# A gated feed-forward behind linear attention on one core: a first strip of 576 tokens, batch 1 by token, and later loads moved by a strip

## The chip, the cores and the metric

The kernel runs on one core of a Trainium2 chip. A core has TensorE (PE in the profile; PEld is its weight load), VectorE (DVE), ScalarE (ACT), GpSimd (POOL) and SyncE (SP), which run side by side and each take their instructions in order. The metric is the device time of one execution in microseconds, as the median of several runs. The profile is of one execution, with times from the start of its span.

## The reference

For each of 8 batches and 8 heads, with 576 tokens of 64 numbers, `kv` sums over the tokens, `q` is multiplied by it, each token's 64 results are divided by their root mean square and scaled by `g_norm`. The eight heads of a token side by side are a row of `x` (4608 x 512). Then comes a gated feed-forward of width 1536.

```python
kv = np.einsum('bhsd,bhse->bhde', k, v)
out = np.einsum('bhsd,bhde->bhse', q, kv)
rms = np.sqrt(np.mean(out * out, axis=-1, keepdims=True) + 1e-06)
attn = out / rms * g_norm
x = attn.transpose(0, 2, 1, 3).reshape(B * S, H * D)
y = ((x @ w_a) * (x @ w_b)) @ w_out
```

## The kernel before, in words

**Feed-forward.** The 4608 tokens are cut into 9 strips of 512. `xt` holds x transposed (channels in the partitions, 4 blocks of 128 channels). In a strip, a unit (class `Unit`, `ffn_ab`) makes 128 of the 1536 columns: 4 products with `wa_t` into one PSUM bank, copied by ACT to `a_sb` (L373), then 4 products with `wb_t` into another bank, which DVE multiplies with the copy into `abt` (L377). Twelve units, n = 0 to 11, are followed by four output groups of 128 tokens, n = 12 to 15 (`ffn_o`): 12 products with `wo_t` each, a copy by DVE or ACT in turn (L431, L429), and stores issued by SP (L409). All products go through `product` (L161), which cuts each into two with 64 columns of weights where `halves` is set.

**Attention.** The 576 tokens of a batch are not aligned with the strips: batch b begins at token 576 b, strip s at 512 s. Batches 0 and 1 (`EARLY`) are loaded by POOL per pair of heads (`load_heads`, L119), with q transposed by PE (`qtr`) and kv made by PE (`kv1`). Their x is made per pair with channels in the partitions: product with q (`px`, or `x` with the block-diagonal `kvb`), square on ACT (`psq`), sum over channels by a product with `ones` and reciprocal root on ACT (`pss`, L233), scaling on DVE into `xt` (`pst`, L243). Batch 0 does this at the head, batch 1 between the half groups of strip 0's output.

**Batches 2 to 7, by token.** `load_late` (L137 to L150) issues six DMAs on POOL: q, in two, to a DRAM tile `qs` in bf16, k and v, each with its last 64 tokens apart. A small copy to `gate` makes POOL wait for the last but one batch's q transpose first. `transpose_q` (L154) is a transposing DMA issued by SP from `qs` to `qT`. PE then makes kv into bank 7 (`kv`, L178, 40 products), a copy gives `kvs` (L618), and `tx` (L293, 40 products) makes x with tokens in the partitions: four chunks of 128 tokens in banks 4 to 7, a last chunk (`LC`) of 64 in two other banks, copied off by ACT (L304). Each chunk then takes `tsq` (square, ACT L310), `tss` (sum over 64, DVE L314), `trs` (reciprocal root on ACT L323, then its product with `g_all` on POOL L330) and `txt` (product, DVE L339, and a transposing DMA on SP into `xt`, L343).

**What sets the order.** The program is written out by hand, and each engine takes its part of it in order. In strip s, `slot(A, s, n)` places the steps of batch s + 1 after unit or group n, and in the middle of it for halves: with k0 = 5, 1, 4, 0, 4, 0 in strips 1 to 6 for kv (in strips 3 and 5 for two batches at once) and x0 = 6.5, 2.5, 5.5, 0.5, 5.5, 0.5 for tx. Loads of a batch are issued two batches ahead at n = 14, 10, 14, 8 of strips 1 to 4; those of batch 2 follow batch 1's at the head, those of batch 3 come at n = 3 of strip 1.

**Loads at the head.** POOL issues batch 0's later pairs, then the weights `wa_t` and `wb_t` in blocks of 256 columns (L477, L130, L131), `wo_t` in 12 pieces (L134), then batch 1's pairs and batch 2. Eight such DMAs are in flight at once; a ninth waits for the first (rows such as "POOL wo_t L134 <- DMA wb_t" in the view of the waits).

## Time and profile before

| what | us |
|---|---|
| median of 3 runs (312.43 to 312.77) | 312.49 |
| profiled execution | 312.61 |
| its span | 310.8 |
| PE busy, first product of the feed-forward to last product | 14.1 to 307.6 |
| strip 0, units | 14.10 to 35.15 |
| strip 0, output groups with batch 1 between | 35.15 to 49.96 |
| strip 1 | 49.96 to 82.75 |
| granted TensorE clock, as a share of full speed | 1.0 |

A line of a timeline gives the start and the duration in us, the engine, the line of the kernel and the operation with what it writes and reads; "x12" is the number of instructions that it merges. Products overlap, so a group's end is some 0.17 us behind the start of the next. In the view of the DMA issues the last number is the time from issue to landing in us. The clock was granted in full in every stretch, so durations may be carried from one stage to another.

### The profile page before, as it was taken

How to read it: one execution, taken by the hardware profiler on the slowest of the kernel's cores; microseconds unless marked ns; L12 is line 12 of the kernel's file. 1: busy time of each engine (PE TensorE's matmuls, PEld its weight loads, DVE VectorE, ACT ScalarE, POOL GpSimd, SP SyncE). 2: the span in 40 equal slices, each digit the busy share in tenths (PEclk: the TensorE clock that was granted, in tenths of full speed). 3: DMA queues.
4: the chain of work that ended last, by engine and by line, in shares of the span. 5: the costliest groups of instructions: out<-in, count | busy, mean ns of one | idle time of the engine just before them, and what ended most of it. 6: DMA issues, size and time to landing. Idle time of an engine off the chain costs nothing.

```text
span 310.8 us, 6542 instructions
## 1 busy us (share of the span) xinstructions
PE 304.3 (98%) x2684; PEld 157.6 (51%) x2701; DVE 140.6 (45%) x235; ACT 117.0 (38%) x231; POOL 101.3 (33%) x123
## 2 busy tenths in 40 slices
PE   7899999999999999999999999999999999999996
PEld 3444476655555555555555555444444444444444
DVE  4544335458248603484386123752782143214321
ACT  3743255354255313551564034632651233123310
POOL 8954991093274630043646300221240000000000
PEclk9999999999999999999999999999999999999999
DMA  8999999999899999047998990073021200030002
GB/s 180 197 196 199 201 188 168 161 169 184 174 137 185 139 174 193 2 84 134 178 177 118 162 188 2 19 160 110 20 51 42 103 1 0 34 103 0 0 36 101
DMA packets 94403, 36.29 MB, mean 117 GB/s; under 512 B 64934, under 2 KB 89894, under 8 KB 94374
## 3 DMA queue, kind: packets, MB, share of 16 engines
q0 software_dynamic: 59120, 18.44, 56.6%
q1 hardware_dynamic: 34786, 16.93, 25.0%
q10 hardware_dynamic: 468, 0.51, 0.6%
q8 instruction: 21, 0.34, 0.5%
q14 instruction: 8, 0.07, 0.1%
HBM read 37.78 MB, written 12.98 MB: 163 GB/s over the span
## 4 chain that ended last, share of the span: by engine, by line
PE 79%; DMA 12%; POOL 7%; issue 1%; ACT 0%; POOLq 0%
PE P L161 77%; DMA wb_t<-in_moe_w_b_dram 6%; DMA vtl<-in_v_dram 4%; DMA wo_t<-in_moe_w_out_dram 2%; PE P L293 1%; PE P L178 1%; POOL vt L119 1%; POOL qt L119 1%; POOL qs L142 1%; POOL kt L119 1%; POOL wa_t L477 0%; POOL wb_t L477 0%; POOL wo_t L134 0%; POOL ktl L145 0%; POOL vtl L145 0%
## 5 line engine op out<-in xcount | busy, mean ns | idle before, releaser
L377 DVE TENSOR_TENSOR ab<-P,asb 128x512 bf16<-128x512 f32 x108 | 74.4, 691 | 103.2 <-PE P L161 99.9
L161 PE MATMUL P<-xt,wb_t 128*64 128x512 bf16 (+1 forms) x641 | 111.4, 379 | 0.2
L161 PE MATMUL P<-xt,wa_t 128*64 128x512 bf16 (+1 forms) x636 | 111.0, 379 | 0.6 <-issue 0.2
L373 ACT CAST asb<-P 128x512 bf16<-128x512 f32 x108 | 63.1, 586 | 89.6 <-PE P L161 89.5
L161 PE MATMUL P<-wo_t,ab 128*64 128x512 bf16 (+3 forms) x673 | 95.5, 371 | 0.3
L161 PEld LDWEIGHTS <-ab 128*64 128x64 bf16 (+1 forms) x678 | 47.5, 106 | 45.0
L161 PEld LDWEIGHTS <-wa_t 128*64 128x64 bf16 (+1 forms) x644 | 46.0, 106 | 46.2 <-issue 0.6
L161 PEld LDWEIGHTS <-wb_t 128*64 128x64 bf16 (+1 forms) x644 | 45.8, 106 | 45.8
L330 POOL TENSOR_TENSOR sqt<-rst,g_all 128x512 f32<-128x512 f32 (+1 forms) x24 | 25.0, 1046 | 83.0 <-ACT rst L323 83.0
L429 ACT COPY osb<-P 128x512 f32<-128x512 f32 x17 | 10.0, 586 | 70.2 <-PE P L161 60.2
L431 DVE COPY osb<-P 128x512 f32<-128x512 f32 x18 | 12.4, 691 | 44.9 <-PE P L161 40.4
L142 POOL DMA_DIRECT2D qs<-in_q_dram x12 | 19.8, 1654 | 0.7 <-issue 0.3
L314 DVE TENSOR_REDUCE sst<-sqt 128x8 f32<-128x512 f32 (+1 forms) x24 | 16.3, 680 | 1.7 <-ACT sqt L310 1.5
L339 DVE TENSOR_TENSOR qv<-P,sqt 128x512 bf16<-128x512 f32 x18 | 12.3, 681 | 0.0
L330 POOL TENSOR_TENSOR k_x<-rst,g_all 128x512 f32<-128x512 f32 x6 | 6.3, 1044 | 17.4 <-ACT rst L323 17.4
L323 ACT ACTIVATE rst<-sst,eps_t 128x8 f32<-128x8 f32 (+1 forms) x30 | 9.0, 300 | 7.2 <-DVE sst L314 7.0
L310 ACT ACTIVATE sqt<-P 128x512 f32<-128x512 f32 x18 | 10.5, 585 | 0.1
L243 DVE SCALAR_TENSOR_TENSOR xt<-P,g_col,rs 128x288 bf16<-128x288 f32 x16 | 7.5, 511 | 5.1 <-ACT rs L233 5.1
L134 POOL DMA_DIRECT2D wo_t<-in_moe_w_out_dram x12 | 6.4, 530 | 6.7 <-DMA wb_t<-in_moe_w_b_dram 3.2
L233 ACT ACTIVATE rs<-P,eps_t 128x576 f32<-128x576 f32 (+1 forms) x9 | 6.1, 689 | 3.7 <-PE P L161 3.4
L139 POOL COPY gate<-qT 1x1 bf16<-1x1 bf16 x5 | 0.9, 177 | 18.9 <-DVE kvs L618 14.0
L444 PE MATMUL P<-zeros 128*128 128x512 bf16 x16 | 5.8, 510 | 1.2 <-DVE eps_t L461 1.2
(72 smaller groups left out, 131.7 us busy)
## 6 DMA issues: line engine op xcount, KB each, us to landing
out_dram<-osb SPq DMA_DIRECT2D x23, 256.0 KB, 2.1
qs<-in_q_dram POOLq DMA_DIRECT2D x12, 288.0 KB, 7.5
ktl<-in_k_dram POOLq DMA_DIRECT2D x6, 512.0 KB, 9.6
vtl<-in_v_dram POOLq DMA_DIRECT2D x6, 512.0 KB, 12.2
out_dram<-osb SPq DMA_DIRECT2D x13, 128.0 KB, 2.4
wo_t<-in_moe_w_out_dram POOLq DMA_DIRECT2D x12, 128.0 KB, 6.0
wa_t<-in_moe_w_a_dram POOLq DMA_DIRECT2D x5, 256.0 KB, 8.9
wb_t<-in_moe_w_b_dram POOLq DMA_DIRECT2D x5, 256.0 KB, 9.5
```

Source lines behind the costliest of these rows:

```text
L119: nc.gpsimd.dma_start(out=t[:, hs, :, :], in_=src[b, hs].rearrange("h (t c) d -> t h c d", c=EC))
L142: nc.gpsimd.dma_start(out=d[:, hs, :], in_=q[b, hs].rearrange("h t d -> t h d"))
L161: nc.tensor.matmul(o[r], lhsT=lhsT[:, r], rhs=rhs, **kw)
L310: nc.scalar.activation(sqt[c % 3][r], self.by_head(c)[r], AF.Square)
L314: nc.vector.reduce_sum(sst[c % 3][r], sqt[c % 3][r].rearrange("t j p d -> t (j p) d"), axis=mybir.AxisListType.X,)
L323: nc.scalar.activation(rst[c % 3][r], sst[c % 3][r], AF.Abs_reciprocal_sqrt, bias=eps_t[r], scale=1.0 / D,)
L330: nc.gpsimd.tensor_mul(sqt[c % 3][r].rearrange("t j p d -> t (j p) d"), rst[c % 3][r].unsqueeze(2).to_broadcast([n, H, D]), g_all[r].unsqu ...
L339: nc.vector.tensor_mul(t[r].rearrange("t (p j) d -> t j p d", j=2), self.by_head(c)[r], sqt[c % 3][r])
L373: nc.scalar.copy(self.t, self.a)
L377: nc.vector.tensor_mul(abt[self.s % 2][self.fc], self.b, self.t)
L429: nc.scalar.copy(t, P[:, i, :])
L431: nc.vector.tensor_copy(t, P[:, i, :])
```

## The change

Strip 0's units work on all 576 tokens of batch 0, 448 in the unit itself and 128 in a new `ffn_end` for two units at once; strip 1's units then have the 448 tokens from 576 to 1023, and the output groups stay at 128 tokens from a common `abt`. Batch 1's transposes and kv move between strip 0's units (after 5, 8, 10, 11), its x is made by token after unit 11, and its chain is written out one step after another. Three of strip 0's output groups run interleaved, piece of `wo_t` by piece. Batch 1's loads stand between those of the weights and ahead of `wo_t`. Batch 2 is loaded behind chunk 3's product of batch 1; batch b + 1 at the very end of strip s = b - 1. In strips from 2 on, kv is at n = 9 and tx at n = 10, in strip 1 at 11 and 12; the last chunks' steps go into the next strip, and `transpose_q` to its n = 2. `halves` is set from unit 5 of strip 0 until kv in strip 6.

```diff
+    CUT = S - 128
-    kvb = sb([128, NP, 128], BF16, "kvb")
-    abt = [[sb([128, STRIP], BF16, f"ab{i}_{f}") for f in range(FC)] for i in range(2)]
+    abt = [sb([128, 2 * STRIP], BF16, f"ab{f}") for f in range(FC)]
...
     def load_late(b):
-        if b > EARLY:
-            nc.gpsimd.tensor_copy(gate, qT[(b - 1) % 2][0:1, 0, 0:1])
+        nc.gpsimd.tensor_copy(gate, qT[(b - 1) % 2][0:1, 0, 0:1])
+        load_late_q(b)
+        load_late_kv(b)
...
     class Unit:
         def __init__(self, s, fc, a, b):
+            self.t0, self.n, self.c0 = {0: (0, CUT, 0), 1: (S, 2 * STRIP - S, S)}.get(
+                s, (s * STRIP, STRIP, s % 2 * STRIP)
+            )
...
+    def ffn_end(fc, i):
+        n = S - CUT
+        t = a_sb[Unit.n % 4][:, 0 : 2 * n]
+        Unit.n += 1
+        for m, w in enumerate((wa_t, wb_t)):
+            for j in range(2):
+                for kc in KORD:
+                    product(
+                        P[:, i, (2 * m + j) * n : (2 * m + j + 1) * n],
+                        w[:, kc, (fc + j) * 128 : (fc + j + 1) * 128],
+                        xt[:, kc, CUT:S],
...
-    for i in range(1, d_ff // WC):
-        load_ab(i * WC, (i + 1) * WC)
+    load_ab(WC, 2 * WC)
+    load_ab(2 * WC, 3 * WC)
+    load_pair(1, 0)
+    load_ab(3 * WC, 4 * WC)
+    hs = [slice(2 * p, 2 * p + 2) for p in range(NP)]
+    load_heads(1, qt[1], q, hs[1])
+    load_heads(1, kt[1], k, hs[1])
+    load_ab(4 * WC, 5 * WC)
+    load_heads(1, vt[1], v, hs[1])
+    load_heads(1, qt[1], q, hs[2])
+    load_ab(5 * WC, 6 * WC)
+    load_heads(1, kt[1], k, hs[2])
+    load_heads(1, vt[1], v, hs[2])
+    load_pair(1, 3)
     for i in range(FC):
         load_o(i)
-    for p in range(NP):
-        load_pair(1, p)
-    load_late(2)
+    nc.sync.dma_start(out=gate_d, in_=wb_t[0:1, KC - 1, 2 * WC - 1 : 2 * WC])
+    nc.sync.dma_start(out=g_all, in_=g_norm.partition_broadcast(128))
...
+    for fc in range(4, FC):
+        if fc == 9:
+            ab_banks.remove(4)
         ffn_ab(0, fc)
+        if fc in (5, 8, 10, 11):
+            halves[0] = True
+            pair((5, 8, 10, 11).index(fc))
+        if fc % 2:
+            ffn_end(fc - 1, (ab_banks[0] if fc == FC - 1 else 6 + fc // 2 % 2))
+    lent = ab_banks[1]
+    A.tx(lent)
+    A.tsq(0)
...
+    A.txt(3)
+    A.tsq(4)
+    A.tss(4)
+    A.trsqrt(4)
+    nc.gpsimd.tensor_copy(gate, x_tok[1][0:1, 0, 0, 0:1])
+    load_late_q(2)
+    load_late_kv(2)
+    A.tg(4, nc.gpsimd)
     transpose_q(2)
+    three = (ab_banks[2], ab_banks[0], ab_banks[1])
+    for fc in range(FC + 2):
+        for g, i in enumerate(three):
+            f = fc - (0, 0, 2)[g]
+            if 0 <= f < FC:
+                o_mm(0, g, i, (f,))
+                if f == FC - 1:
+                    o_out(0, g, i)
+    ffn_o(0, 3)
+    u0 = Unit(1, 0, 4, 5)
+    u1 = Unit(1, 1, 6, 7)
+    c = 256
+    for u in (u0, u1):
+        u.mm(wa_t, KORD, (0, c))
+        u.mm(wb_t, KORD, (0, c))
...
     def slot(A, s, n):
+        k0, x0 = (11, 12) if s == 1 else (9, 10)
+        if n == k0:
+            halves[0] = b < B - 1
+            for p in range(NP):
+                A.kv(p, kb[:, 0, p, :])
+            nc.vector.tensor_copy(A.kvs, kb[:, 0])
...
+        if s == 1:
+            sqs, sums = (0, 0.5, 1, 2, 3), (0.5, 1, 1.5, 3, None)
+            rss, outs = (0.5, 1, 1.5, 3, None), (1.5, 2, 2.5, None, None)
+        else:
+            sqs, sums = (0, 1, 2, 3, 4), (1, 2, 3, 4, 5)
+            rss, outs = (1.5, 2.5, 3.5, 4.5, 5), (2.5, 3, 4, 5, None)
...
+            C = Attn(s)
+            if s == 1 and n == 4:
+                C.txt(LC)
+            elif s == 2:
+                if n == 0:
+                    C.txt(LC - 1)
...
+            elif s > 2 and n == 1:
+                C.txt(LC)
+            if 1 < s and n == 2 and A:
+                transpose_q(b)
+            if n == FC + 3 and b + 1 < B:
+                load_late(b + 1)
```

## The prediction

> **What bounds the kernel now.** I read the busy line of the page first, then the chain that ended last, then the timeline of TensorE (PE) from 35 to 90 us, and then POOL's and SP's timelines with the DMA landings.

> ```profile
> PE 304.3 (98%) x2684; PEld 157.6 (51%) x2701; DVE 140.6 (45%) x235; ACT 117.0 (38%) x231; POOL 101.3 (33%) x123
> PE P L161 77%; DMA wb_t<-in_moe_w_b_dram 6%; DMA vtl<-in_v_dram 4%; DMA wo_t<-in_moe_w_out_dram 2%; PE P L293 1%; PE P L178 1%; POOL vt L119 1%; POOL qt L119 1%; POOL qs L142 1%; POOL kt L119 1%; POOL wa_t L477 0%; POOL wb_t L477 0%; POOL wo_t L134 0%; POOL ktl L145 0%; POOL vtl L145 0%
> ```

> PE works without a gap worth naming from 14.1 us to 307.6 us, so each microsecond taken from its list is won and each new wait on it is lost in full. A 512-column product is 0.2158 us (strips without halves: 10.79 us per 50 products) and 1296 of them make 279.7 of these 293.5 us. The rest is 4.45 us for batch 1's attention between 35.15 and 49.96 us (14.81 less 48 products), some 8.8 us for batches 2 to 7, a wait of 0.24 us for batch 2's kv at 60.4 us, and 0.3 us in the head.

> **What PE gains.** In strip 0 the work of batch 1 repeats per pair of heads; this is one pair and then the by-token form that batch 2 already has:

> ```profile
> 43.31 0.44 PE L161 MATMUL P<-sq,ones 128*64 128x288 bf16 x4
> 43.55 0.44 PE L161 MATMUL P<-qT,kvb 128*64 128x288 bf16 x4
> 43.80 0.45 PE L202 MATMUL P<-ident,qt 96*64 96x96 bf16 x12
> 44.05 0.38 PE L178 MATMUL P<-vt,kt 96*64 96x64 bf16 x12
> ...
> 62.92 1.05 PE L161 MATMUL P<-xt,wa_t 128*64 128x512 bf16 x8
> 63.91 0.76 PE L293 MATMUL P<-kvs,qT 64*128 64x64 bf16 x40
> 64.60 1.05 PE L161 MATMUL P<-xt,wb_t 128*64 128x512 bf16 x8
> ```

> The first two rows start 0.24 us apart and go: 4 pairs x 2 x 0.245 = 1.96 us, and the 0.13 us that one of the sums waited. The transposes and kv stay and only move. One tx is added: from 62.92 + 0.86 to 64.60 is 0.83 us. The wait of 0.24 us for batch 2 goes, since its kv moves from unit 5 of strip 1 to after unit 11. Columns of the products are the same: strip 0 has 448 + 128 per unit instead of 512, strip 1 448. The 96 new 128-column products (ffn_end) and the 16 more from splitting u0 and u1 in strip 1 each bring a weight load; the last 24 products of the kernel have 128 columns and their own loads, and take 1.48 us busy, a last drain of some 0.17 included, so 54 ns each, no more than columns x 0.4215 ns. I take 0, with 0 and +0.7 us (61 ns each) as ends. The head loses cover: the first eight products before xt's last row are 27 ns shorter each, while ACT and DVE (rs, then xt until 16.54 us) are not, which I put at 0.17 us (ends 0 and 0.2).

> [...]

> Sum on PE: -1.96 - 0.13 + 0.83 - 0.24 + 0.17 = **-1.33 us**.

> **The stream of weights.** Batch 1's loads are moved ahead of wo and between the weights. In the trace a 256 KB weight piece lands every 1.34 us, a 144 KB head piece every 0.74, a wo piece every 0.67. Replayed in the new order, the third weight block (columns 768 on) lands at 24.9 (wa) and 26.3 (wb), the fourth at 29.1 and 30.4, the fifth at 33.2 and 34.6, batch 1's last pair at 38.3, wo from 39.0 to 46.4. PE, with 1.51 us per 448-column unit, 0.86 per ffn_end and 0.65 per pair, needs them at 26.9/27.7, 30.8/31.6, 35.3/36.1, 39.0, and wo piece f at 41.3 + 0.65 f, the last at 48. The least slack is 1.1 us, so I cost this at nothing; the three interleaved output groups are that cover. Slower by 5%, it costs up to 1 us. POOL ends its issues at 41.6, before x's first multiply (42.6).

> **What becomes late: x at a strip's end.** A strip's first product reads all its 512 tokens. Per chunk of 128 tokens the chain is ACT square 0.60, DVE sum 0.68, ACT rsqrt 0.30, POOL multiply 1.05, DVE product 0.68, then the transposing DMA, which holds SP 1.2 us:

> ```profile
> L330 POOL TENSOR_TENSOR sqt<-rst,g_all 128x512 f32<-128x512 f32 (+1 forms) x24 | 25.0, 1046 | 83.0 <-ACT rst L323 83.0
> L314 DVE TENSOR_REDUCE sst<-sqt 128x8 f32<-128x512 f32 (+1 forms) x24 | 16.3, 680 | 1.7 <-ACT sqt L310 1.5
> xt<-qv SPq DMA_TRANSPOSE x30, 2.6
> ```

> Landing 2.6 us after its issue, one chunk needs 5.9 us and the engines' queues are in order. After strip 0's tx, 10.36 us of output work follow; chunks 0 and 1 land at 8.7 and chunk 3 at 9.9, needed at 10.4 and 12.1: no wait.
> Strip 1: tx stands after the first output group; PE has 7.77 us left. From tx's end: ACT last copies 0.73, square 0 1.35, sum 0 2.07, square 1 2.93, ACT's output copy 3.43, sum 1 3.65, rsqrt 1 4.0, square 2 4.5, sum 2 5.2, rsqrt 2 5.55, POOL 6.65; DVE copies group 14's output 5.28 to 5.97, product 1 6.55, product 2 7.4. SP has the two stores of group 14 until 6.85, chunk 1's transpose until 8.05, and then issues chunk 2, which lands at 10.65. Strip 2 reads chunk 2 (tokens 1408 to 1535): **+2.9 us**.
> Strip 2: tx follows unit 10, PE has 12.09 us left. DVE sum 1 stands behind the copy of group 12 (ends 5.1), product 1 waits for POOL until 7.15, sum 2 ends 8.45, product 2 stands behind the copy of group 14 and ends 10.9; its transpose lands at 13.55. Strip 3 reads chunk 2: **+1.5 us**. Later strips read only chunks 0 and 1, which land by 10.6.
> Ends for a landing: 2.4 and 4.6 us (both in the trace), so 2.7 to 4.9 and 1.3 to 3.5.

> **What becomes late: the next batch's k and v.** The load stands on POOL behind the multiply of chunk 4. In strips 2 to 5: product 2 10.9, sum 3 11.5, rsqrt 3 11.85, POOL 12.95, product 3 13.7, sum 4 14.3, rsqrt 4 14.65 (ACT), POOL 15.75, first issue 16.05, that is 3.96 us after the strip's end. kv stands after unit 9, 17.26 us into the strip. How long a load takes is told by batch 4:

> ```profile
> 84.77 3.31 POOL L142 DMA_DIRECT2D qs<-in_q_dram  x2
> 90.51 0.72 POOL L149 DMA_DIRECT2D vtl<-in_v_dram  x1
> 95.06 6.17 SPq L154 DMA_TRANSPOSE qT<-qs  x1
> ...
> vtl<-in_v_dram POOLq DMA_DIRECT2D x1, 64.0 KB, 12.9
> ```

> 90.51 + 12.9 - 84.77 = 18.6 us. Batches 3, 5, 6 and 7 took 16.5, 18.8, 16.5 and 19.1. Other traffic shares the engines: batch 3 had 0.65 MB of stores and transposes in it, 3.3 us at the 186 GB/s of its last part, so alone 13.2. Batch 4 had 0.5 MB of stores (2.7 us) and its own q transpose, as the new loads will: 15.9. I take **16.0**, ends 13.2 and 19.1.
> Batch 3 (strip 2): issued 0.55 us before that strip's delayed start, lands 15.5 into it: no wait. Batch 4 (strip 3): the strip starts 1.5 late, so the issue is 2.5 into it, landing 18.5, wait **1.25**. Batches 5, 6, 7 (strips 4 to 6): 3.96 + 16.0 - 17.26 = **2.7 each**. Their q transpose (9.6 us from issue in batch 4, landing 1.3 after v) is under kv 0.63 and unit 10 1.73. Behind the waiting kv on PE stand tx and so every x of the next strip; all of them move with it.
> Also, ACT's rsqrt 4 (14.65) stands ahead of the next strip's first a copy, whose bank unit 1's b needs at 14.68: 0.5 us, inside the kv wait in strips 4 to 6, and **+0.5** in strip 7, which has no kv.

> **What moves at no cost.** SP's two small loads now stand ahead of the first transpose and wait for the second weight block (18.7 us); nothing else is on SP until 44.9. Batch 2's load is issued after strip 0's product 3 (48.7 us); q is down at about 57.7, and its transpose holds SP until 64.8 with strip 0's eight stores behind it, done near 70; their buffers are wanted again at 73, tx(2) too at 73 and kv(2) at 69.8 (landing 48.7 + 16.0 = 64.7). The cover is 3 us; beyond it each late microsecond is a wait of PE.

> **Sum.** 2.9 + 1.5 + 1.25 + 3 x 2.7 + 0.5 = 14.25; less 1.33 is +12.9. The profiled execution was 312.61 us (span 310.8 and 1.8 around it), 0.12 above the median 312.49: 325.5 there, **325.4** as a median, slower by 4%.

> **Rivals.**
> 1. Faster: x and loads arrive in time, PE's list alone decides, 312.5 - 1.3 = 311.2. It needs chunk 2 within 7.8 us of tx in strip 1 and loads under 13.3 us. For it: DVE and ACT are 45% and 38% busy. Against: chunk 2 stands third in line with 5.9 us per chunk. 12%.
> 2. Loads alone on the DMA engines: 13.2 us, no kv wait; the starts remain (4.4) and 0.5 in strips 4 to 7: 312.5 + 4.4 + 2.0 - 1.3 = 317.6. For it: the new loads meet few stores. Against: q's transpose falls into them. 17%.
> 3. Loads as slow as batch 7's 19.1: waits of 19.1 - 0.55 - 17.26 = 1.3 (strip 2), 4.3 (strip 3) and 3 x 5.8: 312.5 + 1.3 + 4.3 + 17.4 + 4.9 - 1.3 = 339. 8%.
> 4. Weights or wo late in strip 0: the forecast and 1 to 5 us. 5%.
> 5. Waits of some 1.3 us in all cancel the gain: 312.5. 3%.
> Forecast, 319 to 334: 55%.

> The range 315.5 to 335.5 leaves out the faster and the equal case and most of the slowest. Within 0.2%, about what a measurement of this kernel can tell, lies case 5: faster 0.12, same 0.03, slower 0.85.

> **What would show it.** In the changed kernel's PE timeline: no sum or kvb products after strip 0, its output groups from 41 to 51 us without a gap; a gap of 3 us ahead of strip 2 and 1.5 ahead of strip 3, released by the transposing DMA; a gap ahead of each kv in strips 3 to 6, released by vtl; loads issued on POOL 4 us after a strip's end. Loads issued earlier, or landing within 13 us, would make it wrong.

## The result and the profile after

The changed kernel takes 339.81 us (median of 4 runs, 335.28 to 341.5), the kernel before beside it 312.46 us (4 runs, 312.35 to 312.77). The ratio is 1.0825, interval 1.0721 to 1.0929: slower by 8% (the ratio is that of the means, and leaves out runs over 1.5% above the fastest of their kernel). The forecast was 325.4 us and its range ended at 335.5; direction and places were right, the size was half. The profiled execution took 339.8 us with a span of 338.0, that is 27.2 more than before's 310.8.

From the page of the changed kernel: the busy line, two rows of the 40 slices (busy tenths of PE, and its granted clock in tenths), and the chain that ended last.

```profile
PE 313.2 (93%) x3142; PEld 177.0 (52%) x3151; DVE 147.5 (44%) x251; ACT 117.5 (35%) x235; POOL 105.5 (31%) x128
...
PE   8899999996997989799988999799988999999996
...
PEclk9999999999799999999997999899997999999999
...
PE 58%; DMA 19%; POOL 10%; DVE 6%; issue 4%; ACT 3%; DVEq 0%; POOLq 0%; ACTq 0%
```

PE fell from 98% to 93% of a longer span, and the chain now runs through transfers, POOL and DVE. The new sign is in the clock row: it was full throughout before, and now has dips, each in or next to a slice in which PE was not full. PE is also *busy* 8.9 us longer (313.2 against 304.3) although its list became shorter: the same products took longer.

The view of PE's waits (us in total, times, longest):

```profile
PE P L184 <- DMA vtl<-in_v_dram: 11.0, 10, 1.6
PE P L167 <- DMA xt<-qv: 3.5, 1, 3.5
PE P L167 <- ACT asb L375: 3.0, 4, 0.8
PE P L167 <- issue: 1.5, 2, 1.3
```

These are the waits that were forecast: kv for v (two waits in each of five strips), strip 2's start for its last chunk, unit 1 of strips 4 to 7 for ACT, strip 3's start ("issue"). Strip 4 shows what comes behind such a wait. PE's timeline, and then the windows around it (bounds, length, busy time of PE, PEld, DVE, ACT, POOL, granted clock, DMA share, GB/s):

```profile
175.43 1.06 PE L167 MATMUL P<-xt,wb_t 128*64 128x512 bf16 x8
177.91 0.32 PE L184 MATMUL P<-vtl,ktl 128*64 128x64 bf16 x8 [1.42 <-DMA vtl<-in_v_dram]
179.20 0.69 PE L184 MATMUL P<-vtl,ktl 128*64 128x64 bf16 x32 [0.97 <-DMA vtl<-in_v_dram]
179.70 1.47 PE L167 MATMUL P<-xt,wa_t 128*64 128x512 bf16 x8
180.91 1.97 PE L167 MATMUL P<-xt,wb_t 128*64 128x512 bf16 x8
182.81 1.10 PE L283 MATMUL P<-kvs,qT 64*128 64x64 bf16 x40
183.84 1.05 PE L167 MATMUL P<-xt,wa_t 128*64 128x512 bf16 x8
```

```profile
178.00:180.00 2.00, 1.02 (x44) 0.83 (x45) 0.06 (x1) 0.00 (x0) 0.00 (x0) 1.00 1.15 172
180.00:182.00 2.00, 2.00 (x14) 1.14 (x12) 0.36 (x1) 0.58 (x1) 0.00 (x0) 0.55 0.04 8
```

The eight halves of a group of products take 0.86 us from start to start. Behind the wait the first group takes 1.21 and the second, which tx follows, 1.90 (0.99 in strip 3, at full clock); the granted clock is 0.55 in this window, in which hardly a transfer runs (8 GB/s). Some 3.4 us on, all is as before. The same stands behind strip 2's start (clock 0.50 from 86 to 88 us), and behind kv in strips 5 and 6 (0.50 at 218 and at 256 us), and not behind the wait of 1.43 us ahead of strip 3 nor behind kv in strips 2 and 3.

The whole difference by PE's timeline (a wait is what start to start exceeds the product's own time, some 0.17 more than the profile's figure):

| term | forecast | measured |
|---|---|---|
| PE's own list | -1.33 | -1.2 |
| start of strip 2 | +2.9 | +3.7 |
| kv in strip 2 | 0 | +2.35 |
| start of strip 3 | +1.5 | +1.43 |
| kv in strip 3 | +1.25 | +2.53 |
| strips 4 to 6, unit 1 and kv | +8.1 | +10.97 |
| strip 7, unit 1 | +0.5 | +0.91 |
| products at half clock | not in it | +6.5 |
| sum | +12.9 | +27.2 |

### The profile page after: what moved, and what is told of

The parts are those of the page before. It is cut to its first block, busy times and chain, and to the rows that moved or that the text cites. A ratio compares the mean times of both kernels' runs of the same rounds, so it can differ in the third digit from the quotient of the medians.

```text
span 338.0 us, 7483 instructions
## 1 busy us (share of the span) xinstructions
PE 313.2 (93%) x3142; PEld 177.0 (52%) x3151; DVE 147.5 (44%) x251; ACT 117.5 (35%) x235; POOL 105.5 (31%) x128
## 4 chain that ended last, share of the span: by engine, by line
PE 58%; DMA 19%; POOL 10%; DVE 6%; issue 4%; ACT 3%; DVEq 0%; POOLq 0%; ACTq 0%
PE P L167 52%; DMA vtl<-in_v_dram 18%; POOL qs L146 3%; POOL sqt L328 3%; DVE sst L305 3%; DVE qv L337 2%; PE P L466 2%; PE P L283 2%; PE P L184 2%; POOL ktl L151 1%; POOL vtl L151 1%; ACT rst L317 1%; POOL ktl L155 1%; PE P L203 1%; DMA xt<-qv 1%
## 5 line engine op out<-in xcount | busy, mean ns | idle before, releaser
L379 DVE TENSOR_TENSOR ab<-P,asb 128x512 bf16<-128x512 f32 (+1 forms) x108 | 73.0, 676 | 118.0 <-PE P L167 108.2
L167 PE MATMUL P<-xt,wa_t 128*64 128x512 bf16 (+7 forms) x829 | 116.5, 361 | 5.3 <-DMA xt<-qv 3.5
L167 PE MATMUL P<-xt,wb_t 128*64 128x512 bf16 (+7 forms) x830 | 116.9, 362 | 3.2 <-ACT asb L375 3.0
L375 ACT CAST asb<-P 128x512 bf16<-128x512 f32 (+1 forms) x108 | 61.4, 573 | 116.7 <-PE P L167 116.3
L167 PEld LDWEIGHTS <-wb_t 128*64 128x64 bf16 (+1 forms) x832 | 57.2, 110 | 43.8 <-issue 7.9
L167 PEld LDWEIGHTS <-wa_t 128*64 128x64 bf16 (+1 forms) x832 | 54.9, 109 | 42.6 <-issue 7.9
L328 POOL TENSOR_TENSOR sqt<-rst,g_all 128x512 f32<-128x512 f32 (+1 forms) x27 | 28.0, 1039 | 145.7 <-ACT rst L317 145.6
L317 ACT ACTIVATE rst<-sst,eps_t 128x8 f32<-128x8 f32 (+1 forms) x35 | 10.5, 299 | 41.0 <-DVE sst L305 40.9
L184 PE MATMUL P<-vtl,ktl 128*64 128x64 bf16 x240 | 5.8, 197 | 11.0 <-DMA vtl<-in_v_dram 11.0
L184 PEld LDWEIGHTS <-ktl 128*64 128x64 bf16 x240 | 5.3, 112 | 13.6 <-issue 13.1
L295 ACT COPY rs<-P 64x256 f32<-64x256 f32 x14 | 4.6, 367 | 11.8 <-PE P L283 11.8
```

Of the source, the lines that this page charges most:

```text
L167: nc.tensor.matmul(o[r], lhsT=lhsT[:, r], rhs=rhs, **kw)
L184: nc.tensor.matmul(o[j * D : (j + 1) * D, :], lhsT=kk[0:n, 2 * p + j, c, :], rhs=vv[0:n, 2 * p + j, c, :], start=(c == 0), stop=(c == len( ...
L317: nc.scalar.activation(rst[c % 3][r], sst[c % 3][r], AF.Abs_reciprocal_sqrt, bias=eps_t[r], scale=1.0 / D,)
L328: eng.tensor_mul(sqt[c % 3][r].rearrange("t j p d -> t (j p) d"), rst[c % 3][r].unsqueeze(2).to_broadcast([n, H, D]), g_all[r].unsqueeze(1 ...
L375: nc.scalar.copy(self.t, self.a)
L379: nc.vector.tensor_mul(abt[self.fc][:, self.c0 : self.c0 + self.n], self.b, self.t)
```

## The experiments

The theory after the result: (a) behind a wait PE runs at half clock for a while, which the forecast did not price; (b) the loads stand too late on POOL and take longer than 16 us because transposes run beside them; (c) the starts of strips 2 and 3 wait for one queue of small steps. The rivals: the slow products come from something else in the change (the halves, the transfers), and the loads are long by themselves. e1 to e4 were run together, then e5 to e8, e9 to e11, and e12.

| run | us, median (range, runs) | ratio to before, interval |
|---|---|---|
| e1_warm | 335.54 (334.59 to 336.13, 4) | 1.0743 (1.0722 to 1.0763) |
| e2_load8 | 325.79 (324.69 to 326.32, 4) | 1.042 (1.0396 to 1.0443) |
| e3_root_next | 322.54 (319.6 to 323.71, 4) | 1.0306 (1.0261 to 1.0351) |
| e4_all | 317.06 (316.13 to 317.51, 5) | 1.0143 (1.0124 to 1.0162) |
| e5_dose_a, e6_dose_b, e9_dose_halves | 323.27, 328.5, 325.42 (one run each) | - |
| e7_q_after_v | 342.86 (338.42 to 345.11, 4) | 1.0888 (1.0843 to 1.0933) |
| e8_fit | 318.4 (316.59 to 320.73, 6) | 1.0196 (1.0162 to 1.023) |
| e10_whole | 342.43 (340.31 to 344.69, 4) | 1.0955 (1.0915 to 1.0994) |
| e11_fit2 | 317.9 (316.13 to 321.03, 6) | 1.0166 (1.0138 to 1.0194) |
| e12_fit3 | 317.08 (316.22 to 319.68, 6) | 1.0164 (1.0136 to 1.0192) |

**e1_warm: products on zeros in the waits.** They write a bank that the next real product starts anew.

```diff
+            if s > 1:
+                dummy(10, 4)
             for p in range(NP):
                 A.kv(p, kb[:, 0, p, :])
...
+            if s == 1 and n == FC + 3:
+                dummy(15, 4)
```

> The changed kernel with idle products of zeros put on PE where it waits: 10 of 512 columns (2.16 us) ahead of kv in strips 2 to 6, 15 (3.24 us) ahead of strip 2. They replace waiting, so all waits end as before. Theory (the clock is halved behind a wait of PE): the granted clock stays at 1.0 and the 6.5 us lost in slow products (1.4 ahead in strip 2, 1.6, 1.8 and 1.8 behind kv in strips 4 to 6) go: 333 us. Rival (the products behind a wait are slow because the loads share the memory then): nothing changes, 338 to 341 us.

Measured: 335.5, 4.3 less than the changed kernel in the median and 2.5 above the theory; the profiled span is 332.8, 5.2 less, and the clock was 1.0. PE's timeline around strip 4's kv:

```profile
175.75 2.11 PE L466 MATMUL P<-zeros 128*128 128x512 bf16 x9 [0.16 <-issue]
177.79 0.99 PE L184 MATMUL P<-vtl,ktl 128*64 128x64 bf16 x40
178.59 1.06 PE L167 MATMUL P<-xt,wa_t 128*64 128x512 bf16 x8
179.46 1.05 PE L167 MATMUL P<-xt,wb_t 128*64 128x512 bf16 x8
```

The wait is about as long as before, but filled, and the two groups behind it are busy for 1.06 and 1.05 us instead of 1.47 and 1.97. That shows (a): of the 6.5 us, 5.2 came back in the profiled execution; the dummies bring small waits of their own (tx in strip 4 waits 0.39 us for q).

**e2_load8: the loads earlier.**

```diff
-            if n == FC + 3 and b + 1 < B:
+            if n == 8 and b + 1 < B:
                 load_late(b + 1)
```

> One edit to the changed kernel: batch b + 1 is put on POOL's list at unit 8 of strip s instead of the strip's end, so it runs as soon as q of batch b is transposed. Theory (kv waits because the load is issued 4 us behind the strip's end): the five waits for v (2.35, 2.53, 2.78, 2.86, 2.56 us) and the slow products behind them (5.2) go, the late starts of strips 2 and 3 and the 0.9 us at unit 1 of strips 4 to 7 stay: 321 to 323 us. Rival (the transfers themselves are the bound, and an earlier load only collides with x's transposes): strips 2 and 3 start later by some us each and 328 to 335 us come out.

Measured: every wait of kv is gone, 14.0 us less in the median, but less than the theory said. The start of strip 2 became longer (PE's timeline, then SP's):

```profile
88.36 1.92 PE L167 MATMUL P<-xt,wa_t 128*64 128x512 bf16 x8 [6.59 <-DMA xt<-qv]
90.04 1.95 PE L167 MATMUL P<-xt,wb_t 128*64 128x512 bf16 x8
```

```profile
81.55 2.50 SPq L341 DMA_TRANSPOSE xt<-qv  x2
```

The transposes of chunks 1 and 2 are issued at the same time as in the changed kernel (81.30), but now the load of batch 3 runs beside them, from 68.29 on, and the second lands some 5.5 us after its issue. So the rival was right in its part: the load among x's steps was paid at the next strip's start, with a wait of 6.59 us where the changed kernel has 3.53.

**e3_root_next: the last chunk's sum and root in the next strip**, out of the load's way on POOL and out of unit 1's on ACT.

```diff
-            if m == sums[c]:
+            if m == sums[c] and c < LC:
                 A.tss(c)
-            if m == rss[c]:
+            if m == rss[c] and c < LC:
                 A.trs(c)
...
             elif s > 2 and n == 1:
+                C.tss(LC)
+                C.trs(LC)
+            elif s > 2 and n == 4:
                 C.txt(LC)
```

> One edit: sum and root of the last chunk (and its product on POOL) go to unit 1 of the next strip in all strips, as strip 2 of the changed kernel has them, and its product with x to unit 4. Theory: ACT no longer holds the first a copy, so the 0.92 us at unit 1 of strips 4 to 7 go (3.7), and the loads start some 3 us earlier, which takes the waits for v in strips 3 to 6 to 0 to 1 us and the slow clock with them: 322 to 327 us. Rival (the wait at unit 1 is not ACT's, loads are bound by the transfers): 336 to 340 us.

Measured: as expected. Unit 1 no longer waits; batch 4's load is issued at 123.03 instead of 125.82 us, and kv waits 2.0 us in all instead of 11.0. One place of one chunk's two small steps is thus worth 17 us of the 27, with the half clock behind kv included; it leaves strip 2's start (3.52 us and half clock), strip 3's (1.25 us), and one wait of 1.57 us for x in strip 1 that no other run has.

**e4_all: the three remedies together**, with kv and tx of batch 2 two units earlier.

```diff
-        k0, x0 = (11, 12) if s == 1 else (9, 10)
+        k0, x0 = 9, 10
-        if s == 1:
-            sqs, sums = (0, 0.5, 1, 2, 3), (0.5, 1, 1.5, 3, None)
-            rss, outs = (0.5, 1, 1.5, 3, None), (1.5, 2, 2.5, None, None)
-        else:
-            sqs, sums = (0, 1, 2, 3, 4), (1, 2, 3, 4, 5)
-            rss, outs = (1.5, 2.5, 3.5, 4.5, 5), (2.5, 3, 4, 5, None)
+        sqs, sums = (0, 0.5, 1, 2, 3), (0.5, 1, 1.5, 3, None)
+        rss, outs = (0.5, 1, 1.5, 3, None), (1.5, 2, 2.5, None, None)
...
-            elif s == 2:
+            elif s > 1:
...
-            elif s > 2 and n == 1:
-                C.txt(LC)
...
-            if n == FC + 3 and b + 1 < B:
+            if n == (12 if s == 1 else 8) and b + 1 < B:
```

> The changed strip 0, with later strips mended: kv after unit 9 and tx after unit 10 also in strip 1, the quick chain of strip 1 in all strips, the last two chunks in the next strip, batch 3's load after group 12 of strip 1 and later loads a strip ahead. Theory (all of the loss sits in the named waits of strips 2 to 7, and strip 0's change is worth 1.3 us): no wait over 0.5 us, 311 to 312.5 us. Rival (x's transposes beside the loads are late whatever the order): starts of strips 2 and 3 late by 1 to 3 us, 314 to 320 us.

Measured: 317.06, some 5 us above the theory and inside the rival's range. One wait of PE was left, ahead of strip 2, and half clock behind it; the load of batch 3 on POOL had begun 7.6 us before:

```profile
84.50 1.92 PE L167 MATMUL P<-xt,wa_t 128*64 128x512 bf16 x8 [2.83 <-issue]
86.18 1.52 PE L167 MATMUL P<-xt,wb_t 128*64 128x512 bf16 x8
```

```profile
76.92 3.30 POOL L146 DMA_DIRECT2D qs<-in_q_dram  x2
```

**e5_dose_a and e6_dose_b: waits by themselves.** The kernel before, with squares on scratch tiles ahead of single units of strips 7 and 8, where nothing but the feed-forward runs.

```diff
     def ffn_ab(s, fc, between=None):
+        for _ in range({(7, 2): 6, (7, 8): 7, (8, 2): 8, (8, 8): 9}.get((s, fc), 0)):
+            nc.scalar.activation(sqt[1], sqt[0], AF.Square)
         u = Unit(s, fc, ab_bank(), 0)
```

> The kernel before, whose PE has no wait in strips 7 and 8, with extra squares on ACT (0.60 us each, on scratch tiles that nothing reads) ahead of four units: 6 ahead of unit 2 and 7 ahead of unit 8 of strip 7, 8 and 9 ahead of the same units of strip 8. ACT is idle 1.14 us between two copies and a copy may be late by some 1.1 us, so PE should wait some 1.3, 1.9, 2.5 and 3.1 us, with no transfer, no attention and no gate near. Theory (a wait of TensorE by itself brings the clock down, behind it some 3.3 us run at half speed and cost 1.4 to 1.8 us): the units behind the longer waits, from some 2 to 2.9 us on, take 3.0 to 3.5 instead of 1.73 us, those behind 1.3 us do not; the time is the waits, 8.8, and 1.5 for each unit that is slow. Rival (the slow products of the changed kernel come from the DMA traffic or the attention beside them): all units 1.73 us, the time 8.8 us above before.

> As the run of 6, 7, 8 and 9 squares, with 9 and 8 in strip 7, 7 and 10 in strip 8: waits of some 3.1, 2.5, 1.9 and 3.7 us at other moments. Theory: 3.1 and 3.7 bring the half clock, 1.9 and 2.5 may or may not, by the moment at which they fall; where the same wait is slow in one of the two runs and not in the other, there is no sharp bound on its length. Rival: no unit is slow, 11.2 us above before.

Measured: waits of 1.66, 2.40, 2.85 and 3.51 us in the one and 3.64, 3.07, 2.19 and 4.17 in the other. Only the last brought slow products; PE's timeline of the second kernel:

```profile
268.59 1.02 PE L161 MATMUL P<-xt,wb_t 128*128 128x512 bf16 x4 [3.07 <-ACT asb L373]
269.45 1.03 PE L161 MATMUL P<-xt,wa_t 128*128 128x512 bf16 x4
...
306.35 1.86 PE L161 MATMUL P<-xt,wb_t 128*128 128x512 bf16 x4 [4.17 <-ACT asb L373]
308.01 0.63 PE L161 MATMUL P<-xt,wa_t 128*128 128x512 bf16 x1
```

So a wait alone did it (that of 4.17 us), with no transfer or attention near, and the rival falls; but the theory's "from 2 to 2.9 us on" was too low for these waits: seven of up to 3.64 us cost their own length and no more.

**e9_dose_halves and e10_whole: is it the halves?** The waits of e5 once more with halves in strips 7 and 8, and the changed kernel with none.

```diff
     def ffn_ab(s, fc, between=None):
+        halves[0] = halves[0] or s == 7
```

```diff
-            halves[0] = True
+            halves[0] = False
...
-            halves[0] = b < B - 1
+            halves[0] = False
```

> The run of 6, 7, 8 and 9 squares once more, but in strips 7 and 8 each product is cut into two with 64 columns of weights, as in the changed kernel's strips 1 to 6; the waits keep their lengths of 1.66, 2.40, 2.85 and 3.51 us, behind which whole products ran at full clock. Theory (what counts is how much of the array has worked, and halves work half of it, so that a shorter wait is enough): units behind 2.4 us and more are slow for some 3.3 us, 1.5 us each: 323.3 + 3 to 4.5 = 326 to 328. Rival (in the changed kernel it is the transfers or the kv products around the wait that do it): all units 1.73 us, 323.3.

> The changed kernel with whole products from end to end, halves never set: the same products, columns and waits. Theory (halves make a short wait enough): no slow products behind the waits of 2.1 to 2.9 us, maybe behind the 3.7 us ahead of strip 2; clock 0.995 to 1.0, 339.8 - 5 to 6.5 = 333 to 335. Rival (the clock falls by the length of the wait alone, or whole products bring another loss of clock): 338 to 342, slow units as before.

Measured: with halves, the waits of 2.20 and 2.91 us stay without effect, and only that of 3.52 brings slow products (1.44 us for the second group behind it):

```profile
289.95 1.05 PE L161 MATMUL P<-xt,wb_t 128*64 128x512 bf16 x8 [2.91 <-ACT asb L373]
290.81 1.06 PE L161 MATMUL P<-xt,wa_t 128*64 128x512 bf16 x8
...
304.02 1.05 PE L161 MATMUL P<-xt,wb_t 128*64 128x512 bf16 x8 [3.52 <-ACT asb L373]
304.88 1.71 PE L161 MATMUL P<-xt,wa_t 128*64 128x512 bf16 x8
```

Without halves the changed kernel is no faster, and slow products stand behind the same waits, kv's pause of 1.98 and 0.84 us in strip 4 among them, and behind kv's in strip 3 as well. The halves theory falls. What stays: behind 4.17 us the clock fell; at 2.66 to 3.7 us without other work it did (2.66 in e8_fit, 2.83 in e4_all, 3.52, 3.53) or did not (2.85, 3.07, 3.47 in e11_fit2, 3.51, 3.64), with no order by length; up to 2.4 us between two products of the feed-forward (2.40 in e5_dose_a) it never did. A pause with the small products of kv or tx inside could do it too: in strips 4 to 6 of the changed kernel 3.2 to 3.5 us lie between the feed-forward's products, and in e7_q_after_v waits of 1.72, 2.06 and 2.31 us, with 0.7 to 1 us of kv or tx behind them, were followed by slow products, one of 2.15 was not.

```profile
81.21:84.63 3.42, 0.40 (x4) 0.00 (x0) 1.28 (x2) 1.59 (x4) 1.42 (x3) 1.00 0.65 153
84.63:88.04 3.41, 2.89 (x14) 1.47 (x16) 0.00 (x0) 0.58 (x1) 3.41 (x3) 0.50 0.88 111
88.04:91.45 3.41, 3.41 (x34) 2.03 (x32) 2.40 (x4) 0.58 (x1) 2.73 (x4) 1.00 1.93 124
```

```profile
249.97:253.38 3.41, 1.56 (x7) 0.62 (x7) 0.00 (x0) 3.24 (x6) 0.00 (x0) 1.00 0.00 0
253.38:256.80 3.42, 1.58 (x8) 0.75 (x8) 1.14 (x2) 2.22 (x4) 0.00 (x0) 1.00 0.00 0
256.80:260.21 3.41, 3.41 (x18) 1.51 (x17) 1.34 (x3) 1.17 (x2) 0.00 (x0) 1.00 0.00 0
...
301.17:304.58 3.41, 1.01 (x5) 0.38 (x4) 0.00 (x0) 3.22 (x7) 0.00 (x0) 1.00 0.00 0
304.58:308.00 3.42, 1.65 (x4) 0.55 (x4) 0.69 (x1) 2.18 (x4) 0.00 (x0) 0.50 0.00 0
308.00:311.41 3.41, 3.19 (x8) 1.18 (x8) 0.69 (x1) 0.59 (x1) 0.00 (x0) 0.50 0.00 0
311.41:314.82 3.41, 3.41 (x17) 1.57 (x16) 1.38 (x2) 0.59 (x1) 0.00 (x0) 1.00 0.00 0
```

The 3.64 us fell on two steps and left PE busy for 1.56 and 1.58 us in them: no half clock. From 14 us on, the 14 traces hold some 1,200 steps at full clock: all 17 in which PE was busy for 1.37 us or less were followed by half clock, none with 1.70 or more was, and of the eleven between 1.43 and 1.58 three were, all with small products of kv or tx in them. A step at half clock was followed by full clock where PE was busy for 2.63 us or more (20 times), and by another at half clock at 2.57 or less (4 times). So by these rows some 2.0 us without products within one step were enough (an estimate: 3.41 less 1.37), and the wait of 3.64 us, which fell on two steps, cost no more than its length; no run places a wait against the steps on purpose.

**e7_q_after_v: the load without q's transpose beside it.** The transpose waits on SP for v.

```diff
     def transpose_q(b):
+        if b > 2:
+            nc.sync.dma_start(out=gate_d, in_=vtl[b % 2][0:1, H - 1, 0, 0:1])
         nc.sync.dma_start_transpose(qT[b % 2], qs_d[b])
```

> The changed kernel with the next batch's q transpose held on SP behind a small DMA that reads the loaded v, so that the transpose no longer falls into the load. What it tells is how long the load takes from its first issue. Theory (the load of 16.5 to 17.1 us in strips 3 to 6 and of 22.1 in strip 2 is long because transposes run beside it): v lands 13.2 to 15 us after the first issue, kv waits only 0 to 1 us, but tx then waits for q, whose transpose starts late and takes 6 to 9 us: some 4 us more per strip there, time 340 to 350. Rival (the load is long by its own descriptors): v lands 16 to 17 us after the issue as in the changed kernel, kv waits 2.5 as there, and the time is some 20 us above the changed kernel's.

Measured: strip 2's load on POOL, from the first to the last of its six DMAs:

```profile
84.81 3.31 POOL L146 DMA_DIRECT2D qs<-in_q_dram  x2
...
90.54 0.73 POOL L155 DMA_DIRECT2D vtl<-in_v_dram  x1
```

The last one's time to landing from the view of the issues, first here, then in the changed kernel (where the last is issued at 90.05 and the first at 84.31):

```profile
vtl<-in_v_dram POOLq DMA_DIRECT2D x1, 64.0 KB, 10.5
```

```profile
vtl<-in_v_dram POOLq DMA_DIRECT2D x1, 64.0 KB, 16.4
```

That is 16.2 us, where the changed kernel took 22.1 with the transpose in it; in strips 3 to 6 it is 16.0, 16.3, 15.7 and 15.0 instead of 17.1, 16.8, 16.9 and 16.5. So q's transpose cost the load 0.5 to 1.5 us in strips 3 to 6, and 5.9 in strip 2, where it runs beside chunk 3's transpose. That one is in this run's load too, so by itself it does not make the 22.1; and in e1_warm and e10_whole, with the same steps, strip 2's load took 18.3 and 19.5, so a part of the 5.9 differs from run to run. The load without q's transpose takes 15.0 to 16.3 us and not 13.2: here the rival is nearer, while the time is the theory's. tx then waits 2.1 to 2.8 us for q in strips 3 to 6, and nothing is won. (The profiled execution took 345.1 us.)

**e8_fit, e11_fit2, e12_fit3: where may the load stand?** e8 is e4_all with batch 3's load at the end of strip 1 (`n == FC + 3`) and the last chunk's root one unit later. e11 has that root, and in strip 1 kv and tx one unit earlier than e4_all; e12 moves these by half a unit and puts every load behind n = 13. First e11 against e4_all, then e12 against e11:

```diff
-        k0, x0 = 9, 10
+        k0, x0 = (8, 9) if s == 1 else (9, 10)
...
                 elif n == 1:
                     C.tss(LC)
+                elif n == 2:
                     C.trs(LC)
-                elif n == 4:
+                elif n == 5:
                     C.txt(LC)
```

```diff
-        k0, x0 = (8, 9) if s == 1 else (9, 10)
+        k0, x0 = (8.5, 9.5) if s == 1 else (9, 10)
...
-            if n == (12 if s == 1 else 8) and b + 1 < B:
+            if n == 13 and b + 1 < B:
```

> The run with all three corrections, with two more: batch 3's load goes to the end of strip 1 (behind chunks 1 and 2 of batch 2 and not beside their transposes), and in strips from 2 on the last chunk's root stands one unit later, behind the copy of unit 2, where ACT does not hold that copy up. Theory (what was left there is the wait of 2.83 us ahead of strip 2, its 1.3 us of half clock, and 0.15 us per strip at unit 3): all three go, 317.1 - 2.8 - 1.3 - 0.9 = 312.1, clock 1.0, equal to before or 0.2% faster. Rival (the transposes land late by SP's queue and not by the load beside them): the wait ahead of strip 2 stays above 1.5 us, 314 to 316.

> The run with all three corrections, its kv(2) and tx(2) one unit earlier in strip 1 (after units 8 and 9), so that batch 3's load stands behind the multiply of chunk 3 and the transposes of chunks 1 and 2 have landed when it starts, and the last chunk's root one unit later in strips from 2 on. Theory (the load of batch 3 beside those transposes made the wait of 2.83 us ahead of strip 2, and later than here it makes kv(3) late): chunk 2 lands near 79.5, the load is issued near 79 and lands by 98, no wait is left, clock 1.0: 311.5 to 312.5, equal to before or 0.3% faster. Rival (load and transposes still collide, or kv(2) comes too late): 1 to 4 us of waits, 313 to 317.

> The run before it with kv(2) and tx(2) half a unit later in strip 1 (8.5 and 9.5), and every load behind unit or group 13, that is behind chunk 3's multiply on POOL and after the transposes of chunks 1 and 2. Theory (a load issued among x's steps costs the next strip's start, by POOL's 6.3 us of issues ahead of the multiplies and by traffic beside the transposes; issued 1.3 us ahead of a strip's end it lands in 17 us, 1.6 us before kv wants it): no wait of over 1 us is left, that of 3.47 us ahead of strip 3 and those of 0.73 and 0.58 us in strip 1 go, kv(3) may wait 0.7: 312.5 to 313.5. Rival (a load that late takes 19 us again beside the last chunks' transposes): kv waits of 1 to 2 us in each of strips 2 to 6, 316 to 322.

Measured: all three missed. In e8 strip 2 starts without a wait, which shows that batch 3's load made e4_all's; and the pitch of the later strips falls from 32.69 to 32.53 us, the 0.15 that was expected of the root. But the load now lands after 19.4 us, kv(3) is 0.64 late, the gate opens late for batch 4 (100.79 us), its issues stand on POOL ahead of the multiplies, and strip 3 waits 2.66 us. In e11 the same wait is 3.47 us (half clock did not follow). In e12 no strip waits at its start, the clock is 1.0, and kv waits again:

```profile
PE P L184 <- DMA vtl<-in_v_dram: 3.4, 6, 0.9
PE P L466 <- DVE eps_t L483: 1.2, 1, 1.2
PE P L167 <- ACT sq L226: 0.4, 1, 0.4
PE P L167 <- DVE xt L244: 0.2, 1, 0.2
```

So the rivals of e11 and e12 were nearer: a load among x's steps costs the next strip's start, one behind them costs kv. e12's span without its waits (314.4 less 4.6, worked out from the strips' pitches against 32.53 and kv's wait in strip 2) is 309.8, 1.0 below before's 310.8: by this estimate the shorter list is there, and it is all that the change gains in any of these runs. No version ran faster than the kernel before.

## Why the prediction was wrong, point by point

- **The gain** held: strip 1's products end 1.3 us earlier than before, against 1.33. The weights came in time, and strip 0's output ran without a gap from 40.9 to 51.4 us.
- **"each new wait on it is lost in full"** is the step that failed first. A wait was priced at its own length; four of the waits also cost 1.4 to 1.8 us of half clock behind them, 6.5 us in all (e1_warm, e6_dose_b). Before's trace had no wait that could show it: its longest from 14 us on is under 0.25 us.
- **"I take 16.0"** failed next. 15.0 to 16.3 is what the load takes without q's transpose (e7_q_after_v); with it, as the forecast meant it, it took 16.5 to 17.1 in strips 3 to 6, and 22.1 in strip 2, where q's transpose ran beside chunk 3's. There "no wait" became 2.35 us. The issue came 0.25 us later than worked out. Together 6.4 us: 2.35 in strip 2, 1.28 in strip 3, 2.87 in strips 4 to 6, less 0.07 at strip 3's start. Either of these two steps alone would have given some 332 us; together they make nearly all of the miss.
- **Strip 2's start**, +2.9, was 3.7: DVE's product 0 stood ahead of sum 2, which the list of steps had left out, so root 2 and all behind it came 0.65 us later. Strip 3's, +1.5, was 1.43.
- **ACT in unit 1**: 0.92 instead of 0.5 us; inside kv's wait in strips 4 to 6, as said, and in the open in strip 7.
- The rival with loads of 19.1 us gave 339, close to the result, by another way: it had 4.3 and 3 x 5.8 us for kv where 2.53 and 3 x 3.66 were measured, and no loss of clock. Its opposite, loads of 13.2 us, had no room: 0.65 MB at 186 GB/s are 3.5 us and not 3.3, and the shortest load of all these runs took 14.5 us (e8_fit).

## What to carry to other kernels

In this case, which PE bounds, a new wait of some 2.0 us or more (the estimate above) had 0 to 1.8 us of slow products behind it, by how it fell on the steps of 3.41 us, and more in e6_dose_b, where the clock stayed down for two steps (304.58 to 311.41 us); pauses of 3.2 to 3.5 us with small products of kv in them had them too in strips 4 to 6 of the changed kernel. Price a new wait with such a range. A load took 15.0 to 16.3 us without q's transpose beside it and 16.5 to 22.1 with it, so carry its duration over only with what ran beside it: list the transposes and stores that will fall into it in its new place, and ask which step it will stand ahead of on its own queue. Moving a load here traded one wait for another (2.66 us ahead of strip 3 in e8_fit, 3.4 us at kv in e12_fit3), and the list's gain, 1.2 us, was the bound on the result.

## What the runs showed of the hardware

Transposing DMAs and loads took longer beside each other. A chunk's transpose landed 2.4 us after its issue in the median of the changed kernel and 2.6 in that of before; beside a load it took 5.5 (e2_load8) and 9.4 us (chunk 3 in strip 2 of the changed kernel), and q's transpose rose from a median of 6.6 us before to 10.2; the loads, in turn, took 0.5 to 5.9 us longer with q's transpose in them (e7_q_after_v):

```profile
qT<-qs SPq DMA_TRANSPOSE x6, 10.2
```

128-column products with a weight load each ran at 0.45 us per eight, 56 ns each (the changed kernel's `ffn_end`):

```profile
17.72 0.61 PE L167 MATMUL P<-xt,wa_t 128*128 128x128 bf16 x8
18.17 0.61 PE L167 MATMUL P<-xt,wb_t 128*128 128x128 bf16 x8
```

What stays open is why three of the eleven steps with PE busy for 1.43 to 1.58 us were followed by half clock and eight not.
